# A three-stage fp32 kernel: one pass less when float64 weights are rebuilt, a narrower last product, a new instruction order

## The chip, the cores and the metric

The kernel runs on one core of one Trainium2 chip. Times are device microseconds (us) of one launch. The kernel before takes 1330.62 us, the median of three runs (1329.71 to 1330.99).

## What is computed

Tokens (2 x 4096, 192 channels, float32) pass through three stages:

```
w   = softmax(weight, axis=-1)                # 8 heads, 7 taps
x   = causal_conv(x, w)                       # tap k of head h on its 24 channels
x   = (sigmoid(x @ w_gate) * (x @ w_val)) @ w_out            # 192 -> 1536 -> 192
h   = x @ w_in                                                # 192 -> 2048
P   = a0 + a1*h + a2*h*h + a3*h*h*h
Q   = 1 + |b0|*|h| + |b1|*h*h
out = (P / (Q + 1e-6)) @ w_out2                               # 2048 -> 192
```

The five weight matrices reach the kernel as float64. The result has nearly float32 precision, so each matrix product is made of several TensorE products: both operands are split into a high part (what the fast float32 format fp32r keeps) and a low part (the rest).

## The kernel before, in words

The tokens are cut into 16 tiles of 512. For each tile:

- `conv` makes the seven taps, on POOL for tiles 1 to 15, for tile 0 on TensorE (`conv_first`, 128 channels) and DVE (the other 64), and splits the result into high and low parts (`xha`, `xla`, `xhb`, `xlb`).
- `moe1` makes 12 pairs of 128-row blocks of gate and value. Each block is five TensorE products (`mm192`, L642 to L646: 192 = 128 + 64 channels, high and low parts). ACT applies the sigmoid, DVE multiplies (L688), and for two blocks together (128x1024) `hi1` makes the high part (a copy to fp32r, mostly on ACT) and `lo1` the low part (a subtraction on DVE, L373). Five more products a block, `mm_out` (L649 to L653), add it to `accb`. Of its second accumulator, rows 0 to 63 are the last 64 output channels from the high part of the weight and rows 64 to 127 those from its low part; L653 multiplies that stationary operand with the low part of the data.
- `moe2` makes 16 blocks of `h` with `mm192`; ACT makes `a3*h + a2` (L362, `f<-w,av`) and `|h|`, DVE the polynomial (L753, L755), POOL the denominator's factor (L758), DVE the denominator (L763). The reciprocal is `sigmoid(-log z)`: ACT works on pairs of 128x1024 pieces, first Ln on both, then Sigmoid on both, with a table load on either side. DVE multiplies (L776), `hi2` and `lo2` split, `mm_out` adds to `accd`.

A tile is 340 products of 512 columns (120 + 60 + 80 + 80); 16 tiles make 5440. Ahead of them stand 24 products with zeros (`warm_up`, L599) and the 7 of `conv_first` (L587).

Beside the first tile, 32 pieces of weights are rebuilt. `to_f32` loads pairs of 32-bit words by DMA; ACT rounds the low word's three bits (L444); ACT takes the high word as a float, scales it by 2^-112 and drops its sign (`Abs`); DVE puts the sign bit and the three bits together (L453); DVE shifts the scaled word left by three and puts those bits in (L456). Then a high part (ACT) and a low part (DVE: L373, for the output weights L506 and L508) are made.

The order on every engine is fixed at build time. `Plan` lists the operations with a cost and a priority (`at`: place in time plus an offset by class, `PRM["off"]`), and `Plan.order` goes through model time: the engine that can start soonest takes the operation first in priority. `lock` marks operations of DVE and POOL that the model never lets run at the same time (its shared SBUF port). `alts` lets `hi1`, `hi2` and some copies go to POOL or DVE, with a handicap.

Of the kernel before, what the change touches and what calls it, by code (L numbers as in the profile page):

```python
# [45 lines left out]
class Buf:  # L46
    """A buffer of a kind: the plan gives it a slot, and its first writer its tile."""
# [19 lines left out]
class Plan:  # L67
    """Lists the operations with the buffers that they read and write, then orders them per engine."""
# [6 lines left out]
    def op(self, eng, cost, prio, emit, rd=(), wr=(), table=None, lock=False, alts=()):  # L75
        """alts: other engines that may take the operation, as (eng, cost, emit, lock, handicap)."""
# [32 lines left out]
    def free_slots(self, kind, sort):  # L109
        """Slots of a kind with the time from which each is free, soonest first."""  # L110
# [13 lines left out]
    def fit(self, o):  # L124
        """When the buffers that the operation is first to use can be had, and their slots."""
# [14 lines left out]
    def order(self, look, switch):  # L140
        """In time: the engine that can go on soonest takes, of the operations that it could start
        about then, the one first in priority."""
# [14 lines left out]
        for _ in self.ops:  # L157
            best = None
            for eng in ENGINES:
                found = []  # L160
                for i, o in enumerate(avail[eng]):
                    start = begin(o, eng)
                    if len(o.opts) > 1:
                        ends = {e: begin(o, e) + v[0] + v[3] for e, v in o.opts.items()}
                        if ends[eng] > min(ends.values()):
                            continue
                    found.append((start, o.prio + (switch if o.table and o.table != table else 0.0), i, o))
                found.sort(key=lambda e: e[:3])
                pick, first = None, None
                for start, prio, _, o in found:  # L170
# [14 lines left out]
            o, places, eng = best[1:]  # L185
# [9 lines left out]
            if lock:  # L195
                lock_free = o.end
# [15 lines left out]
        "A": 126, "A.f": -163042, "A.s": 2377, "A.m": 1099, "A.l": 15462, "B": 21954, "B.f": -6649,  # L212
        "B.s": 267339, "B.m": -381, "B.l": 18954, "C": 13792, "C.f": 6615, "C.s": -4092, "C.m": -4326,
        "C.l": -729, "D": 71951, "D.f": 10387, "D.s": -10039, "D.m": 44935, "D.l": 16426, "_": -500387,
        "_.f": -1455, "_.s": -2238, "_.m": -1032, "cb": 85990, "cb.s": 42092, "cb.m": 221, "cb.l": -24842,
        "cv": 108441, "cv.f": 43336, "cv.s": 41633, "cv.l": 5162, "g": -205204, "g.f": -5118, "g.s": 25353,
        "g.m": -7291, "g.l": -9696, "gv": -295099, "gv.f": -7488, "gv.s": 2254, "gv.m": 2921, "ha": 16691,
        "ha.f": -13423, "ha.s": 193315, "ha.m": -32839, "ha.l": 821, "hi1": -34492, "hi1.f": -586,
# [7 lines left out]
        "u.s": 53322, "u.m": -21400, "u.l": 5206, "v": 95617, "v.f": -5614, "v.s": 40813, "v.m": -6140,
        "v.l": 22160, "w": 16438, "w.f": -155676, "w.l": 46096, "wA": -67088, "wA.f": -16171, "wA.s": 4804,
        "wA.m": -6466, "wA.l": -16824, "wB": -72573, "wB.f": 31019, "wB.s": 8326, "wB.m": 53803,
        "wB.l": 1311, "wC": -84679, "wC.s": 22921, "wC.m": 34154, "wC.l": 40145, "wD": 115730,
        "wD.f": 5940, "wD.s": -20677, "wD.m": -48332, "wD.l": 27289, "xs": -442528, "xs.f": -16231,  # L230
# [30 lines left out]
def at(cls, t, x):  # L261
    """Priority of an operation of a class for tile t: its place x in time, moved as the class is."""
# [9 lines left out]
def conv_gated_rational_kernel(  # L272
# [113 lines left out]
    def small():  # L386
# [14 lines left out]
        # exp(z) as sigmoid(z) / sigmoid(-z)  # L401
# [16 lines left out]
        # |b[0]| has a floor far below the rounding of 1, so that the logarithm below stays finite  # L418
# [16 lines left out]
    def to_f32(cls, prio, nbytes, n, load, k=1):  # L435
        """n float64 per partition, as pairs of words, to float32."""
        raw, t = Buf("f", "raw"), Buf("f", "t")

        def words():
# [3 lines left out]
        # the low word's three bits of the float32, rounded  # L443
# [6 lines left out]
        # the high word, its exponent field cut from 11 bits to 8  # L450
        act(at(cls, None, prio + 1), n, lambda: T(t)[:, 0:n], lambda: f(words()[:, :, 1]), [raw], [t],
            func=ACTF.Abs, scale=2.0 ** -112)
        dve(at(cls, None, prio + 2), n, lambda: nc.vector.scalar_tensor_tensor(  # L453
            out=words()[:, :, 0], in0=words()[:, :, 1], scalar=-2 ** 31, in1=words()[:, :, 0],
            op0=ALU.bitwise_and, op1=ALU.bitwise_or), [raw, (raw, 0)], [(raw, 0)])
        dve(at(cls, None, prio + 3), n, lambda: nc.vector.scalar_tensor_tensor(  # L456
            out=T(t)[:, 0:n].bitcast(I32), in0=T(t)[:, 0:n].bitcast(I32), scalar=3, in1=words()[:, :, 0],
            op0=ALU.logical_shift_left, op1=ALU.bitwise_or), [t, (raw, 0)], [t])
        return t

    def split_rows(cls, prio, src, c0, n, hi, lo, key):
        """Columns c0..c0+n of the first 128 rows of a [192, ff] weight."""
# [396 lines left out]
```

## Time and profile before

| what | value |
|---|---|
| median of three runs | 1330.62 us |
| span of the profiled execution, first to last instruction | 1328.7 us |
| PE products, share of the span | 1285.7 us, 97% |
| PE weight loads (overlap the products) | 1032.1 us, 78% |
| DVE | 1238.4 us, 93% |
| ACT | 1162.2 us, 87% |
| POOL | 634.7 us, 48% |
| ACT table loads | 127 of 1.283 us |

The profile gives the span of its execution and no separate time for it. The median of the three runs is 1.9 us above that span; this is what lies around it. A product is pipelined, so the duration of one (about 0.39 us) is longer than the distance from one to the next, and the busy share of PE alone does not say how many products were made. The product count of a stretch, times the distance between two products that do not wait, does.

### The profile page before, as it was taken

What the parts mean: (1) busy time and instruction counts of PE and PEld (TensorE: products, weight loads), DVE (VectorE), ACT (ScalarE), POOL (GpSimd) and SP (SyncE); (2) the same over time, 40 slices, a digit from 0 to 9 for tenths busy, and PEclk for the clock granted to TensorE, in tenths of its full rate; (3) what the DMA queues carried; (4) which work ended last, traced back from release to release, by engine and by line L of the source; (5) the groups of instructions that cost most, each with busy time, mean ns of one, the idle gap of its engine ahead of it and who ended that gap; (6) DMA issues with size and microseconds to landing.
All of it is one profiled execution on the core that took longest, in us unless ns stands there. A gap on an engine that the chain in (4) does not pass through costs nothing.

```text
span 1328.7 us, 15322 instructions
## 1 busy us (share of the span) xinstructions
PE 1285.7 (97%) x5478; PEld 1032.1 (78%) x5478; DVE 1238.4 (93%) x1429; ACT 1162.2 (87%) x1545; POOL 634.7 (48%) x440
## 2 busy tenths in 40 slices
PE   7899799999999999999999999999999999999996
PEld 3767588887888888888888887788888788888874
DVE  8999999999999999999988999999999999999997
ACT  5888889888998889898898889988989888999897
POOL 4035464676355562666517563374644656122222
PEclk8899899999999999999999999999999999999999
DMA  5510100000000000000000000000000000000000
GB/s 166 169 52 25 52 0 21 0 21 9 8 13 1 24 13 1 12 9 21 9 9 5 8 21 9 12 1 17 13 9 13 0 21 1 1 12 1 13 12 12
DMA packets 14316, 27.08 MB, mean 20 GB/s; under 512 B 2080, under 2 KB 5792, under 8 KB 14240
## 3 DMA queue, kind: packets, MB, share of 16 engines
q1 hardware_dynamic: 14240, 26.11, 6.8%
q8 instruction: 43, 0.70, 0.2%
q14 instruction: 33, 0.27, 0.1%
HBM read 19.81 MB, written 6.29 MB: 20 GB/s over the span
## 4 chain that ended last, share of the span: by engine, by line
PE 76%; DVE 14%; ACT 8%; issue 2%; DMA 0%; SPq 0%; DVEq 0%; ACTq 0%
PE w L642 9%; PE w L643 9%; PE w L644 9%; PE w L645 9%; PE w L646 9%; ACT f L362 5%; PE accd L651 4%; PE accd L653 4%; PE accd L652 4%; PE accd L650 4%; PE accd L649 3%; PE accb L651 3%; PE accb L653 3%; PE accb L652 3%; PE accb L649 3%; PE accb L650 3%
## 5 line engine op out<-in xcount | busy, mean ns | idle before, releaser
L758 POOL TENSOR_SCALAR f<-f,bv 128x1024 f32<-128x1024 f32 x128 | 199.0, 1555 | 535.9 <-ACT f L362 479.5
L373 DVE TENSOR_TENSOR r<-f,r 128x1024 fp32r<-128x1024 f32 x224 | 293.2, 1324 | 5.6 <-PE accb L653 1.6
L362 ACT ACTIVATE f<-f 128x1024 f32<-128x1024 f32 (+3 forms) x288 | 285.0, 1004 | 2.8 <-DVE f L763 1.6
L362 ACT ACTIVATE f<-w 128x512 f32<-128x512 f32 x448 | 257.2, 595 | 29.3 <-PE w L646 14.5
L362 ACT ACTIVATE f<-w,av 128x512 f32<-128x512 f32 x256 | 196.7, 774 | 61.5 <-PE w L646 47.6
L362 ACT ACTIVATE r<-f 128x1024 fp32r<-128x1024 f32 x203 | 214.3, 1058 | 26.0 <-DVE f L688 19.8
L755 DVE SCALAR_TENSOR_TENSOR f<-f,av,w 128x512 f32<-128x512 f32 x256 | 187.5, 743 | 8.7 <-ACT f L362 4.4
L753 DVE TENSOR_TENSOR f<-f,w 128x512 f32<-128x512 f32 x256 | 170.7, 680 | 23.0 <-ACT f L362 22.0
L763 DVE SCALAR_TENSOR_TENSOR f<-f,f 128x1024 f32<-128x1024 f32 x128 | 187.9, 1471 | 0.8 <-POOL f L758 0.5
L776 DVE SCALAR_TENSOR_TENSOR f<-f,av,f 128x1024 f32<-128x1024 f32 x128 | 170.4, 1348 | 8.0 <-ACT f L362 7.8
L362 ACT ACT_TABLE_LOAD x126 | 161.7, 1283 | 2.5 <-DVE r L373 0.3
L688 DVE TENSOR_TENSOR f<-f,w 128x512 f32<-128x512 f32 x192 | 130.7, 681 | 23.8 <-PE w L646 13.5
L569 POOL TENSOR_TENSOR ca<-ca,tmp 128x512 f32<-128x512 f32 x90 | 145.5, 1616 | 6.3
L566 POOL TENSOR_SCALAR tmp<-xa,cw 128x512 f32<-128x512 f32 x90 | 124.4, 1382 | 5.5 <-DMA xa<-in_xt 0.5
L651 PE MATMUL accd<-r,wo_s 128*128 128x512 f32 x256 | 102.3, 400 | 5.4 <-DVE r L373 5.3
L650 PE MATMUL accd<-r,wo_s 128*128 128x512 f32 x256 | 101.5, 396 | 4.4 <-DVE wo_s L508 4.4
L649 PE MATMUL accd<-r,wo_s 128*128 128x512 f32 x256 | 101.3, 396 | 3.4 <-ACT r L362 3.3
L642 PE MATMUL w<-yha,w_h 128*128 128x512 f32 x256 | 101.4, 396 | 3.0 <-ACT f L362 2.0
L652 PE MATMUL accd<-r,wo_s 128*128 128x512 f32 x256 | 101.3, 396 | 0.0
L653 PE MATMUL accd<-r,wo_s 128*128 128x512 f32 x256 | 101.3, 396 | 0.0
L644 PE MATMUL w<-yla,w_h 128*128 128x512 f32 x256 | 100.5, 393 | 0.0
L645 PE MATMUL w<-yhb,w_b 128*128 128x512 f32 x256 | 100.4, 392 | 0.0
(104 smaller groups left out, 2861.4 us busy)
## 6 DMA issues: line engine op xcount, KB each, us to landing
f<-in_wo SPq DMA_DIRECT2D x14, 384.0 KB, 3.3
xa<-in_xt SPq DMA_DIRECT2D x16, 259.0 KB, 2.8
out_dram<-f SPq DMA_DIRECT2D x16, 256.0 KB, 2.0
xb<-in_xt SPq DMA_DIRECT2D x16, 129.5 KB, 2.8
f<-in_w SPq DMA_DIRECT2D x4, 512.0 KB, 3.9
out_dram<-f SPq DMA_DIRECT2D x16, 128.0 KB, 2.3
f<-in_wg SPq DMA_DIRECT2D x4, 256.0 KB, 4.2
f<-in_wv SPq DMA_DIRECT2D x4, 256.0 KB, 4.7
```

What stands on the lines that cost most here:

```text
L362: plan.op("ACT", (53 if psum else 95) + n * 0.832 + 93 * ptr, prio, lambda: nc.scalar.activation(out=out(), in_=in_(), func=func, **kw), r ...
L373: dve(prio, n, lambda: nc.vector.tensor_tensor(out=out(), in0=in0(), in1=f(in1()), op=ALU.subtract), rd, wr, lock=lock, alts=alts)
L642: nc.tensor.matmul(o, lhsT=wh.tile[:, c], rhs=ha, start=True, stop=False)
L644: nc.tensor.matmul(o, lhsT=wh.tile[:, c], rhs=la, start=False, stop=False)
L645: nc.tensor.matmul(o, lhsT=wb.tile[:, c], rhs=hb, start=False, stop=False)
L650: nc.tensor.matmul(a1, lhsT=w[:, 2, :], rhs=h, start=False, stop=False)
L651: nc.tensor.matmul(a1, lhsT=w[:, 0, :], rhs=l, start=False, stop=last)
L652: nc.tensor.matmul(a2, lhsT=w[:, 1, :], rhs=h, start=first, stop=False)
L653: nc.tensor.matmul(a2, lhsT=w[:, 1, :], rhs=l, start=False, stop=last)
L755: dve(at("w", t, p), sn, lambda q=q, cut=cut, h=h: nc.vector.scalar_tensor_tensor(out=cut(u[q]), in0=cut(u[q]), scalar=av.tile[:, 1:2], in ...
L758: plan.op("POOL", 328 + 0.832 * gn, at("n", t, p), lambda q=q: nc.gpsimd.tensor_scalar(C(n[q]), C(ha[q]), bv.tile[:, 1:2], bv.tile[:, 0:1] ...
L763: dve(at("y", t, p), gn, lambda q=q: nc.vector.scalar_tensor_tensor(out=C(n[q]), in0=C(ha[q]), scalar=1e-9, in1=C(n[q]), op0=ALU.max, op1= ...
```

## The change

1. `to_f32`: the scaling of the high word is by `Prelu` in place of `Abs`, with alpha = -2^32. A negative word becomes positive and its exponent gets 32 more, a bit that the shift by three moves into the sign's place. DVE's pass L453 falls away, 32 instructions; L456 of before (L461 now) puts in the rounded bits straight from the low word.
2. `mm_out`: the fifth product of a block has 96 stationary columns in place of 128 (416 of the 448; the last block of each accumulation keeps 128). The 32 rows left out would get low part times low part.
3. The order: the model's products take 0.4473 ns a column at full clock in place of 0.422, its shared port is given back 120 ns (DVE) or 140 ns (POOL) before an operation ends and goes to who asked first, and the offsets, handicaps and look-aheads have other values.

The diff, cut (lines taken out of it hold comments and docstrings, and the offsets, whose rows say nothing by themselves):

```diff
+FREES = dict(DVE=120.0, POOL=140.0)
...
-            step = 0.422 if self.cols.get(w - 1, 0.0) >= BUSY else 0.8386
+            step = 0.4473 if self.cols.get(w - 1, 0.0) >= BUSY else 0.8386
...
-                        pick = (key, start, o, places, eng)
-                if pick is not None and (best is None or pick[1] < best[0]):
+                        pick = (key, start, max(asked, t), o, places, eng)
+                if pick is not None and (best is None or pick[1:3] < best[0:2]):
...
             if lock:
-                lock_free = o.end
+                lock_free = max(o.start, o.end - FREES[eng])
...
-    look=dict(PE=0, ACT=0, DVE=19, POOL=31839, SP=0),
-    switch=403355,
+    look=dict(PE=0, ACT=0, DVE=0, POOL=1791, SP=1611),
+    switch=665544,
...
-        hi1=dict(DVE=90316, POOL=72271), hi2=dict(DVE=2766, POOL=113), lo1=dict(POOL=92669),
+        hi1=dict(DVE=380786, POOL=62531),
+        hi2=dict(DVE=73, POOL=0),
+        lo1=dict(POOL=603097),
...
         act(at(cls, None, prio + 1), n, lambda: T(t)[:, 0:n], lambda: f(words()[:, :, 1]), [raw], [t],
-            func=ACTF.Abs, scale=2.0 ** -112)
+            func=ACTF.Prelu, scale=2.0 ** -112, alpha=-2.0 ** 32)
         dve(at(cls, None, prio + 2), n, lambda: nc.vector.scalar_tensor_tensor(
-            out=words()[:, :, 0], in0=words()[:, :, 1], scalar=-2 ** 31, in1=words()[:, :, 0],
-            op0=ALU.bitwise_and, op1=ALU.bitwise_or), [raw, (raw, 0)], [(raw, 0)])
-        dve(at(cls, None, prio + 3), n, lambda: nc.vector.scalar_tensor_tensor(
             out=T(t)[:, 0:n].bitcast(I32), in0=T(t)[:, 0:n].bitcast(I32), scalar=3, in1=words()[:, :, 0],
-            op0=ALU.logical_shift_left, op1=ALU.bitwise_or), [t, (raw, 0)], [t])
+            op0=ALU.logical_shift_left, op1=ALU.bitwise_or), [t, raw], [t])
...
-        nc.tensor.matmul(a2, lhsT=w[:, 1, :], rhs=l, start=False, stop=last)
+
+        m = 128 if last else 96
+        nc.tensor.matmul(a2[0:m], lhsT=w[:, 1, 0:m], rhs=l, start=False, stop=last)
...
-                    plan.op("PE", pe(tn), at("D", t, base + j * Pt / M2), lambda j=j, k=k, c=c: mm_out(
+                    plan.op("PE", pe(tn, 4.943), at("D", t, base + j * Pt / M2), lambda j=j, k=k, c=c: mm_out(
```

How the instructions move is seen in their order on each engine. First DVE at its start, around its first weight passes (`cb` is the convolution of the 64 channels, `wo_s` output weights, `wg_l` the low part of the gate's weights, `f` work buffers). Before:

```order
L453 SCALAR_TENSOR_TENSOR f_129<-f_129 128x256
L561 SCALAR_TENSOR_TENSOR cb_137<-xb_115,cw,cb_137 128x512
L506 TENSOR_TENSOR wo_s<-f_154,wo_s 128x2x64
L508 TENSOR_TENSOR wo_s<-f_154,wo_s 128x2x128
L561 SCALAR_TENSOR_TENSOR cb_137<-xb_115,cw,cb_137 128x512
L456 SCALAR_TENSOR_TENSOR f_158<-f_158,f_129 128x256
L453 SCALAR_TENSOR_TENSOR f_134<-f_134 128x256
L453 SCALAR_TENSOR_TENSOR f_140<-f_140 128x256
L373 TENSOR_TENSOR xlb_187<-cb_137,xhb_179 64x512 x2
L373 TENSOR_TENSOR xla_197<-w_143,xha_191 128x512
L373 TENSOR_TENSOR wg_l<-f_158,wg_h 128x256
```

Now:

```order
L461 SCALAR_TENSOR_TENSOR f_143<-f_143,f_126 128x256
L461 SCALAR_TENSOR_TENSOR f_157<-f_157,f_129 128x256
L566 SCALAR_TENSOR_TENSOR cb_137<-xb_115,cw,cb_137 128x512
L381 TENSOR_TENSOR wg_l<-f_143,wg_h 128x256
L381 TENSOR_TENSOR wg_b<-f_157,wg_b 64x256
L461 SCALAR_TENSOR_TENSOR f_167<-f_167,f_135 128x256
L381 TENSOR_TENSOR wv_b<-f_157,wv_b 64x256
L566 SCALAR_TENSOR_TENSOR cb_137<-xb_115,cw,cb_137 128x512
L381 TENSOR_TENSOR wv_l<-f_167,wv_h 128x256
```

The gate's first low part was the 28th row of DVE's list and is the 17th; the first piece of output weights went ahead of it and now comes behind the first pieces of gate and value. The loads on SP's queue changed places in the same way.

Next PE, at a block of `mm_out` in the first tile (`r` are the high and low parts of the data). Before:

```order
L650 MATMUL accb_354<-r_335,wo_s 128x512
L651 MATMUL accb_354<-r_345,wo_s 128x512
L652 MATMUL accb_355<-r_335,wo_s 128x512
L653 MATMUL accb_355<-r_345,wo_s 128x512
L649 MATMUL accb_354<-r_335,wo_s 128x512
```

Now:

```order
L655 MATMUL accb_340<-r_308,wo_s 128x512
L656 MATMUL accb_340<-r_321,wo_s 128x512
L657 MATMUL accb_341<-r_308,wo_s 128x512
L660 MATMUL accb_341<-r_321,wo_s 96x512
L654 MATMUL accb_340<-r_308,wo_s 128x512
```

The product with 96 columns stands in the place of L653, in front of a product with 128.

Last ACT, at a pair of Ln early in the run (in-place `f` of 128x1024 is Ln behind one table load and Sigmoid behind the next; `f<-w` without `av` is a sigmoid of the gate or an absolute value). Before:

```order
L362 ACT_TABLE_LOAD
L362 ACTIVATE f_1395<-f_1395 128x1024
L362 ACTIVATE f_1468<-w_1513,av 128x512
L362 ACTIVATE f_1491<-f_1491 128x1024
L362 ACTIVATE f_1502<-w_1513 128x512
L362 ACT_TABLE_LOAD
```

Now:

```order
L370 ACT_TABLE_LOAD
L370 ACTIVATE f_1447<-f_1447 128x1024
L370 ACT_TABLE_LOAD
L370 ACTIVATE f_1504<-w_1538 128x512
L370 ACTIVATE f_1567<-w_1528,av 128x512
L370 ACTIVATE f_1572<-w_1528 128x512
L370 ACT_TABLE_LOAD
L370 ACTIVATE f_1477<-f_1477 128x1024
```

A gate's sigmoid now stands between the two Ln of this pair, with a table load on either side; this happens in 14 pairs, so that ACT has 155 table loads in place of 127. Counted over the whole order, ACT makes 170 high parts of 128x1024 in place of 203, POOL 40 in place of 21, and DVE 14 in place of none.

## Rows read from the trace of the kernel before

**Rows 1.** Page, part 1: busy us, share of the span, instructions of each engine.

```profile
PE 1285.7 (97%) x5478; PEld 1032.1 (78%) x5478; DVE 1238.4 (93%) x1429; ACT 1162.2 (87%) x1545; POOL 634.7 (48%) x440
```

**Rows 2.** Windows: length, busy us (instructions) of each engine, granted clock, DMA.

```profile
17.00:180.00 163.00, 140.93 (x547) 108.70 (x547) 154.81 (x212) 131.69 (x212) 70.96 (x51) 0.92 0.27 79
...
22.00:24.00 2.00, 2.00 (x6) 1.52 (x6) 2.00 (x4) 1.77 (x5) 1.86 (x2) 0.50 1.05 365
...
180.00:1270.00 1090.00, 1086.30 (x4721) 884.19 (x4721) 1022.87 (x1137) 973.88 (x1257) 549.68 (x375) 1.00 0.04 10
1270.00:1328.70 58.70, 45.05 (x175) 33.66 (x173) 49.01 (x56) 47.99 (x59) 13.34 (x9) 0.94 0.05 14
```

**Rows 3.** Timeline of PE from 600 us: start us, us, engine, line, instruction.

```profile
600.21 0.39 PE L652 MATMUL accb<-r,wo_s 128*128 128x512 f32 x1
...
611.65 0.39 PE L652 MATMUL accd<-r,wo_s 128*128 128x512 f32 x1
```

**Rows 4.** Waits of PE, 17 to 180 us: us in total, times, longest.

```profile
PE accd L650 <- DVE wo_s L508: 4.4, 1, 4.4
...
PE accb L651 <- DVE r L373: 2.7, 2, 1.4
```

**Rows 5.** Groups by line and form, DVE, 0 to 200 us: busy, mean ns | idle before.

```profile
L453 DVE SCALAR_TENSOR_TENSOR f<-f 128x384 int32<-128x384 int32 x14 | 11.1, 817 | 0.0
L453 DVE SCALAR_TENSOR_TENSOR f<-f 128x512 int32<-128x512 int32 x12 | 9.5, 811 | 0.0
...
L453 DVE SCALAR_TENSOR_TENSOR f<-f 128x256 int32<-128x256 int32 x6 | 3.2, 562 | 0.0
```

**Rows 6.** Line L453: ns min/median/max, first and last start.

```profile
L453 DVE SCALAR_TENSOR_TENSOR f<-f x32: 423/680/1786, 9.8 to 175.8; 128x384 int32<-128x384 int32 x14, 128x512 int32<-128x512 int32 x12, 128x256 int32<-128x256 int32 x6
```

**Rows 7.** Timeline of DVE, from 9.8 us.

```profile
9.77 0.56 DVE L453 SCALAR_TENSOR_TENSOR f<-f 128x384 int32<-128x384 int32 x1
10.23 0.75 DVE L561 SCALAR_TENSOR_TENSOR cb<-xb,cw,cb 128x512 f32<-128x512 f32 x1
```

**Rows 8.** Timeline of PE's weight loads: products with bf16 zeros, at full clock.

```profile
4.94 0.31 PEld L599 LDWEIGHTS <-zeros 128*128 128x128 bf16 x2
...
7.31 0.31 PEld L599 LDWEIGHTS <-zeros 128*128 128x128 bf16 x2
```

**Rows 9.** The same, fp32r products at half clock.

```profile
22.16 0.33 PEld L645 LDWEIGHTS w<-xhb,wv_b 128*128 128x128 f32 x1
...
23.87 0.33 PEld L644 LDWEIGHTS w<-xla,wg_h 128*128 128x128 f32 x1
```

**Rows 10.** Lines L653 and L599: ns min/median/max of the weight loads.

```profile
L653 PEld LDWEIGHTS accd<-r,wo_s x256: 187/188/330, 119.6 to 1323.2; 128*128 128x128 f32 x128
...
L599 PEld LDWEIGHTS <-zeros x24: 98/98/151, 1.3 to 7.7; 128*128 128x128 bf16 x24
```

**Rows 11.** Line L362 on ACT, 180 to 1270 us: ns min/median/max.

```profile
L362 ACT ACTIVATE f<-w x389: 575/596/645, 185.5 to 1269.4; 128x512 f32<-128x512 f32 x195
...
L362 ACT ACTIVATE f<-w,av x226: 752/777/814, 183.9 to 1269.9; 128x512 f32<-128x512 f32 x113
```

**Rows 12.** Timeline of ACT in the tail.

```profile
1304.58 1.04 ACT L362 ACTIVATE f<-f 128x1024 f32<-128x1024 f32 x1
1305.64 1.28 ACT L362 ACT_TABLE_LOAD   x1
1306.93 2.01 ACT L362 ACTIVATE f<-f 128x1024 f32<-128x1024 f32 x2
```

**Rows 13.** Line L358 on POOL, and two groups by line of DVE.

```profile
L358 POOL TENSOR_SCALAR r<-f x21: 1044/1053/1914, 162.5 to 1311.4; 128x1024 fp32r<-128x1024 f32 x21
...
L373 DVE TENSOR_TENSOR r<-f,r 128x1024 fp32r<-128x1024 f32 x224 | 293.2, 1324 | 5.6 <-PE accb L653 1.6 <-PE accb L652 1.1 <-ACT f L362 0.8
...
L558 DVE TENSOR_SCALAR cb<-xb,cw 128x512 f32<-128x512 f32 x1 | 0.5, 488 | 2.3 <-DMA xb<-in_xt 2.3
```

**Rows 14.** Waits of ACT, 180 to 1270 us.

```profile
ACT f L362 <- PE w L646: 52.9, 66, 2.6
```

More of the change, by code (lines that the diff above doesn't have):

```diff
@@ L166, in order @@
                             continue
-                    found.append((start, o.prio + (switch if o.table and o.table != table else 0.0), i, o))
+                    found.append((start, o.prio + (switch if o.table and o.table != table else 0.0), i, o,
+                                  max(free[eng], o.ready)))
                 found.sort(key=lambda e: e[:3])
                 pick, first = None, None
-                for start, prio, _, o in found:
+                for start, prio, _, o, asked in found:
                     if first is not None and start > first + look[eng]:
@@ L211 @@
     off={
[L212 to L216, printed above, removed]
@@ L226 @@
[L226 to L230, printed above, removed]
@@ L231 @@
-        "xs.s": 13914, "xs.m": -15171, "xs.l": -39981, "y": -355208, "y.f": -7695, "y.s": 1663,
-        "y.m": 24499, "ye": -431004, "ye.f": -15550, "ye.s": 821, "ye.m": 9621, "ye.l": 20452,
-        "late": -1636,
-    },
-    look=dict(PE=0, ACT=0, DVE=19, POOL=31839, SP=0),
-    switch=403355,
+        "A": -639, "A.f": -1063628, "A.s": 3849, "A.m": -5402, "A.l": 20648, "B": 24359, "B.f": 101,
+        "B.s": 722765, "B.m": -6951, "B.l": 152716, "C": 10166, "C.f": 10448, "C.s": 11168, "C.m": -1283,
@@ new lines @@
+        "C.l": -258574, "D": 70387, "D.f": -2028, "D.s": -614, "D.m": 1145112, "D.l": -70882, "_": -500387,
+        "_.f": -1455, "_.s": -2238, "_.m": -1032, "cb": 77111, "cb.s": 42092, "cb.m": 106261, "cb.l": -24842,
+        "cv": 141808, "cv.f": 43336, "cv.l": 41643, "g": 930, "g.f": 58060, "g.s": -73181, "g.m": -13081,
+        "g.l": -42561, "gv": -280594, "gv.f": -114326, "gv.s": 107189, "gv.m": -100720, "ha": 62917,
+        "ha.f": 87796, "ha.s": 256, "ha.m": -14101, "ha.l": 381418, "hi1": -87178, "hi1.f": -6018,
[4 rows of a table added]
@@ new lines @@
+        "n.l": 199703, "oe": 102172, "oe.f": -59209, "oe.s": -590, "oe.m": 47437, "oe.l": 152139, "r": 171267,
+        "r.f": -146955, "r.s": 18933, "r.l": 76895, "sig": -27281, "sig.f": -741190, "sig.s": -143913,
+        "sig.m": -3296, "sig.l": 100824, "u": 731, "u.f": 2963, "u.s": 20903, "u.m": 589, "v": 266828,
+        "v.f": -61171, "v.s": 29097, "v.m": 35890, "v.l": -18955, "w": -98481, "w.f": 16961, "w.l": 47711,
+        "wA": -104549, "wA.f": -16171, "wA.s": 4804, "wA.m": -6466, "wA.l": -16824, "wB": -95021,
@@ new lines @@
+        "wB.f": 31019, "wB.s": 8326, "wB.m": 53803, "wB.l": 1311, "wC": -86460, "wC.s": 22921, "wC.m": 34154,
+        "wC.l": 40145, "wD": 515662, "wD.f": 5940, "wD.s": -20677, "wD.m": -48332, "wD.l": 27289,
+        "xs": -656637, "xs.f": 544, "xs.s": 4476, "xs.m": 7392, "xs.l": 440853, "y": -620020, "y.f": 9273,
+        "y.s": 1832, "y.m": -58874, "ye": -212572, "ye.s": 103292, "ye.m": 164438, "ye.l": -156589,
+        "late": 9141, "ld.f": -2869, "lo2.s": -448302, "gv.l": -86635, "w.s": -107106, "cb.f": 23472,
@@ L237 @@
+        "cv.m": -98167, "y.l": -369111, "w.m": 30924, "hi2.f": -154, "ln.l": -3795, "ld.l": 342338,
+        "r.m": -95445,
+    },
+    look=dict(PE=0, ACT=0, DVE=0, POOL=1791, SP=1611),
+    switch=665544,
     slots=dict(f=12, r=7, y=1),
@@ L239 @@
     alt=dict(
-        hi1=dict(DVE=90316, POOL=72271), hi2=dict(DVE=2766, POOL=113), lo1=dict(POOL=92669),
-        lo2=dict(POOL=17018), n=dict(DVE=86223), round=dict(DVE=34164),
-        xy=dict(DVE=67223, POOL=15669),
+        hi1=dict(DVE=380786, POOL=62531),
+        hi2=dict(DVE=73, POOL=0),
+        lo1=dict(POOL=603097),
+        lo2=dict(POOL=222218),
+        n=dict(DVE=1362960),
+        round=dict(DVE=1027190),
+        xy=dict(DVE=562408, POOL=308632),
     ),
@@ L695, in moe1 @@
                 c = slice(i % g * n, (i % g + 1) * n)
-                plan.op("PE", pe(n), at("B", t, base + i * Pt / M1), lambda i=i, h=h, l=l, c=c: mm_out(
+                plan.op("PE", pe(n, 4.943), at("B", t, base + i * Pt / M1), lambda i=i, h=h, l=l, c=c: mm_out(
                     T(a1)[:, 0:n], T(a2)[:, 0:n], wo_s.tile[:, i], T(h)[:, c], T(l)[:, c], i == 0, i == M1 - 1),
```

7 lines of the change are left out of this document (1 added, 6 removed), and 8 rows, old and new, of the table off.

## The prediction

> **What bounds the kernel now.** The page's first part [rows 1] says PE 97%, DVE 93%, ACT 87%: three engines near full, so the share does not decide, and a busy PE may be waiting inside a product. The timeline of PE in an undisturbed stretch [rows 3] gives the distance between products: 50 products from 600.21 to 611.65 us, 0.229 us each. With it the windows [rows 2] tell the time lost in a stretch, its length less products times 0.229. From 17 to 180 us 547 products need 125.3 of 163 us: 37.7 us lost. From 180 to 1270 us 4721 products need 1081 of 1090: 9 lost. From 1270 us to the end 175 need 40.1 of 58.7: 18.6 lost. So the middle is bound by PE, and the losses lie in the head, where the weights are rebuilt, and in the tail, where the last tile's chain runs out.
>
> In the head DVE is busy 154.8 of 163 us [rows 2] and the longest waits of PE there end with it: a low part of the output weights, a low part of the data [rows 4]. Each loss also pulls the clock down (mean granted share 0.92 there against 1.00 in the middle [rows 2]). What DVE need not do before a product, PE gets back; and as the middle is PE's, what is gained in the head stays gained to the tail.
>
> **One pass less.** L453 runs 32 times, 14, 12 and 6 by size, for 11.1 + 9.5 + 3.2 = 23.8 us [rows 5], all between 9.8 and 176 us [rows 6]: the whole pass lies in the head, on the engine that bounds it. Not all of it need come back. The mean of 0.81 us for 512 elements holds waiting in front of POOL's work; the median of all is 0.68, the least 0.42 [rows 6], and the next instruction starts 0.10 before one ends (0.56 us long, next start after 0.46 [rows 7]). Undisturbed, the passes cost 14 x 0.46 + 12 x 0.58 + 6 x 0.32 = 15.3 us. ACT's pass stays one pass: Sigmoid and Abs share the group `f<-w` and all of it lies between 575 and 645 ns [rows 11], so I cost Prelu in Abs's place at nothing. If its alpha were fetched as the two per-partition operands of `f<-w,av` are, it would cost as much as 777 - 596 = 181 ns a pass, 32 x 0.18 = 6 us, on an ACT that is idle 31 of 163 us there [rows 2]. The low word now waits for two ACT passes of its own piece only, and nothing stands between.
>
> **The order in the head.** Counted in the two orders, the rows that DVE must issue for a low part in front of a given product fall from 182 to 159 (about 445 products in), from 201 to 172 (about 510), from 266 to 236 (about 700), from 278 to 254 (about 770) and from 338 to 304 (about 970). These 23 to 34 rows hold the passes removed and some work put off (output weights of the second layer). At 154.8 / 212 = 0.73 us a row they are 17 to 25 us. The first weights also come earlier: the gate's low part is DVE's 17th row, was the 28th; on SP's queue its load is ahead of the output weights' first. I take 22 us. The lower end is 12: the 15.3 us less some 3 that DVE will now idle, as ACT and the loads are nearer behind it. The upper end is 28: the 25 us with some of the time that the half clock cost; PE can't get back more than 37.7.
>
> **The 96 columns.** An fp32r weight load takes 188 ns at full clock, a bf16 one 98 [rows 10]. The bf16 products follow each other after (7.31 - 4.94) / 11 = 0.2155 us [rows 8], the fp32r ones after 0.229 [rows 3]. At half clock (1.2 GHz; granted share 0.50 from 22 to 24 us [rows 2]) the fp32r load takes 0.33 and its products come after (23.87 - 22.16) / 4 = 0.43 us [rows 9], which is 512 columns at 1.2 GHz. So the extra 13.5 ns show only where load plus some 40 ns is longer than the stream of columns: the load sets the distance. From half to full clock it falls by 330 - 188 = 142 ns, the part that goes with the clock; a quarter fewer columns take 36 ns off, 188 + 41 - 36 = 193 ns, below 215.5. So the distance in front of each of 416 products becomes 0.2155: 416 x 0.0135 = 5.6 us. Ends: 0, if the 13.5 ns belong to fp32r streams and not to loads, and 5.6. No row shows a product of fewer columns; that it could cost more than one of 128 has nothing for it in the trace. [...]
>
> **The middle.** ACT gets 28 more table loads. A load takes 1.28 us, starts 0.02 us after the instruction before it ends and the next starts 0.01 after it [rows 12]: 1.29 us, 28 x 1.29 = 36 us. 33 high parts of some 0.95 us leave ACT, 31 us. Net 5 us of the 116 in which ACT is idle between 180 and 1270 us [rows 2]; it waits there for PE for 52.9 us [rows 14], so it has time. The Trainium skill, "ScalarE: Activation LUTs", section "What ACT_TABLE_LOAD costs", counts 1.38 us of draining on top of 1.28 for each switch; by it 28 switches would be 39 us more of ACT, and the rival of the split pairs below would cost up to 75 us, not 36. The trace shows no such gap. DVE gets 14 copies of 1024 elements, of between 0.49 us (512 elements, L558) and 1.32 (L373 at 1024) [rows 13], 7 to 18 us, I take 9, and the 17 to 25 us put off or brought nearer by the head: some 31 of its 67 idle us [rows 2]. POOL gets 19 copies of 1.05 us [rows 13], 20 us, in 540 idle ones. All three still fit, but with less play; I take 3 us more lost, between 0 and 12.
>
> **The tail.** ACT is busy 48.0 and DVE 49.0 of 58.7 us [rows 2]. Both orders reach the last tile's fifth block after the same 5275 products; from there ACT has 64 rows where it had 66, DVE the same kinds. Behind the last block's products PE has 60 `mm_out` products left, had 70. I take 1 us less, between 5 less and 4 more.
>
> **Sum.** -22 - 5.6 + 3 - 1 = -25.6. The profiled span of 1328.7 becomes 1303.1, and with the 1.9 us that the median lies above it, 1305.0 us.
>
> **Rivals.**
> *The head stays bound* (12 us gained, not 22): ACT and the loads take DVE's place. Against it: ACT is busy 131.7 of 163 us there [rows 2], 81%. For it: each weight piece is a chain of load, two ACT passes, DVE, ACT, DVE, and a shorter DVE shows the rest. 1305 + 10 = 1315 us.
> *The narrow product gives nothing*: 1305 + 5.6 = 1310.6 us. For it only that no row shows fewer columns.
> *The split pairs of Ln reach PE*: in 14 pairs the second Ln comes behind a gate's sigmoid and two loads, so two reciprocals, their high and low parts and 20 `mm_out` products come 2.6 us later or more. If PE paid the 28 loads in full, 36 us: 1341 us, slower than before. It decides when PE pays over 25.6 of the 36, about 0.9 us a load. Against it: between 180 and 1270 us PE has other blocks to go on with, it lost 9 us in all there with 114 loads.
> *The rest*: an order whose model fits better also loses less in the middle and the tail, 1290 us or below; or DVE's put-off work comes up short in the middle, 1320 us and more.
>
> **How the numbers follow.** Forecast, 0.58, its own range 1295 to 1313. Head still bound 0.16. Nothing from the 96 columns 0.10. Split pairs reach PE 0.06 (of it 0.04 slower than before). The rest 0.10, 0.05 on either side. The range of eight in ten takes the forecast with its ends, the narrow product's rival and most of the first: 1291 to 1320. A measurement of this kernel tells some 0.2%, 2.7 us, from no change. Faster by more: all but what lies above 1328, 0.92. Within: 0.03. Slower: 0.05.
>
> **What would show it.** Right: between 17 and 180 us over 620 products in place of 547; no L453; the distance in front of the 96-column product 0.215 to 0.217 us and a load of some 0.15 us; 155 table loads with waits of PE between 180 us and the tail of under 12 us; a tail as long as before. Wrong in the head: fewer than 600 products there, with DVE no longer at 95% and waits of PE that end with ACT or a DMA. Wrong on the columns: 0.229 in front of L660. Wrong altogether: waits of PE behind ACT in the middle that sum to more than 25 us.

## The result, and the profile after

The changed kernel takes 1338.95 us, median of four runs (1337.27 to 1340.15); the kernel before, beside it, 1330.16. The ratio is 1.0065, 95% interval 1.0051 to 1.0079: slower by 0.65%, where 1305 us was forecast. The profiled execution's span is 1336.5 us.

The page's first part, answering to [rows 1]:

```profile
PE 1299.0 (97%) x5478; PEld 1017.2 (76%) x5478; DVE 1220.8 (91%) x1411; ACT 1166.3 (87%) x1540; POOL 661.1 (49%) x459
```

The windows, answering to [rows 2] (length, busy us and instructions of PE, PEld, DVE, ACT, POOL, granted clock, DMA):

```profile
17.00:180.00 163.00, 153.41 (x640) 119.04 (x641) 154.96 (x203) 141.57 (x224) 91.75 (x66) 0.99 0.26 76
180.00:1270.00 1090.00, 1078.70 (x4596) 852.96 (x4596) 999.54 (x1124) 964.07 (x1232) 546.70 (x374) 1.00 0.03 10
1270.00:1336.50 66.50, 53.18 (x206) 39.73 (x204) 55.99 (x62) 51.74 (x64) 21.88 (x14) 0.90 0.04 12
```

The head did what was forecast: 640 products in place of 547, 93 x 0.229 = 21.3 us, with DVE as busy as before. The loss is in the middle: 4596 products in place of 4721, at the full clock. With the prediction's measure, length less products times 0.229, the middle now loses 1090 - 1052.5 = 37.5 us, where it lost 9.

Two things fill these 37.5 us. PE's timeline shows the first (start us, us, engine, line, instruction):

```profile
399.89 0.40 PE L657 MATMUL accb<-r,wo_s 128*128 128x512 f32 x1
400.13 0.40 PE L660 MATMUL accb<-r,wo_s 128*96 128x512 f32 x1
400.36 0.40 PE L647 MATMUL w<-yha,w_h 128*128 128x512 f32 x1
...
402.46 0.40 PE L660 MATMUL accd<-r,wo_s 128*96 128x512 f32 x1
```

and the timeline of its weight loads:

```profile
399.89 0.16 PEld L660 LDWEIGHTS accb<-r,wo_s 128*96 128x96 f32 x1
400.13 0.19 PEld L647 LDWEIGHTS w<-yha,w_h 128*128 128x128 f32 x1
```

From 399.89 to 402.46 us are 11 distances, 0.2336 each, in place of 0.229 [rows 3]. The narrow load is shorter as forecast (0.16 us against 0.19), but its product starts no earlier: 0.24 us behind the one before. And every other product, all of 128 columns, is later too.

The second is waits. In the waits of DVE between 180 and 1270 us (us in total, times, longest) stands after the change

```profile
DVE f L760 <- ACT f L370: 37.4, 47, 3.5
DVE f L695 <- ACT f L370: 13.1, 17, 2.4
```

and before it

```profile
DVE f L753 <- ACT f L362: 22.0, 42, 1.3
...
DVE f L688 <- ACT f L362: 6.4, 11, 1.4
```

L760 is L753 of before, the polynomial's first multiplication, and L695 is L688, the gate's. To set the two apart, all starts of products were counted in PE's order: distances under 0.25 us are running (their excess over 0.229 is "distance"), those of 0.40 to 0.432 are half clock, and the excess of the rest is "waits". Each of these columns has the value before and after.

| products | before | after | distance | half clock | waits |
|---|---|---|---|---|---|
| 0 to 38 (start) | 15.3 | 17.6 | -0.2, -0.2 | 4.0, 4.5 | 2.8, 4.5 |
| 38 to 700 (head) | 189.8 | 166.3 | 0.1, 1.5 | 8.7, 1.4 | 29.4, 11.8 |
| 700 to 5282 (middle) | 1058.5 | 1086.9 | -0.2, 15.9 | 0.0, 0.0 | 9.4, 21.7 |
| 5282 to 5477 (tail) | 58.5 | 59.0 | 0.1, 0.4 | 1.8, 3.0 | 12.0, 11.0 |

The sum is +2.3 - 23.5 + 28.4 + 0.5 = +7.7 us; the spans differ by 1336.5 - 1328.7 = 7.8.

### The profile page after: what moved, and what is told of

Read it like the earlier page. It is cut to its first block, busy times and chain, and to the rows that moved or that the text cites. A ratio compares the mean times of both kernels' runs of the same rounds, so it can differ in the third digit from the quotient of the medians.

```text
span 1336.5 us, 15377 instructions
## 1 busy us (share of the span) xinstructions
PE 1299.0 (97%) x5478; PEld 1017.2 (76%) x5478; DVE 1220.8 (91%) x1411; ACT 1166.3 (87%) x1540; POOL 661.1 (49%) x459
## 4 chain that ended last, share of the span: by engine, by line
PE 44%; DVE 23%; ACT 22%; issue 6%; POOL 3%; DMA 0%; SPq 0%; ACTq 0%; DVEq 0%; POOLq 0%
ACT f L370 13%; PE w L647 5%; PE w L651 5%; PE w L649 5%; PE w L648 5%; PE w L650 5%; DVE r L381 4%; ACT L370 4%; DVE f L760 4%; DVE f L762 4%; DVE f L783 3%; DVE f L770 3%; ACT r L370 3%; PE accd L656 2%; DVE f L695 2%
## 5 line engine op out<-in xcount | busy, mean ns | idle before, releaser
L765 POOL TENSOR_SCALAR f<-f,bv 128x1024 f32<-128x1024 f32 x128 | 185.1, 1446 | 482.0 <-ACT f L370 375.8
L381 DVE TENSOR_TENSOR r<-f,r 128x1024 fp32r<-128x1024 f32 x224 | 299.0, 1345 | 7.9 <-PE accd L660 2.4
L760 DVE TENSOR_TENSOR f<-f,w 128x512 f32<-128x512 f32 x256 | 172.0, 681 | 42.7 <-ACT f L370 42.1
L370 ACT ACTIVATE r<-f 128x1024 fp32r<-128x1024 f32 x170 | 179.0, 1058 | 35.9 <-DVE f L695 22.7
L762 DVE SCALAR_TENSOR_TENSOR f<-f,av,w 128x512 f32<-128x512 f32 x256 | 188.8, 744 | 13.3 <-ACT f L370 9.0
L770 DVE SCALAR_TENSOR_TENSOR f<-f,f 128x1024 f32<-128x1024 f32 x128 | 178.2, 1393 | 7.3 <-POOL f L765 7.3
L783 DVE SCALAR_TENSOR_TENSOR f<-f,av,f 128x1024 f32<-128x1024 f32 x128 | 176.6, 1392 | 8.2 <-ACT f L370 7.9
L695 DVE TENSOR_TENSOR f<-f,w 128x512 f32<-128x512 f32 x192 | 130.5, 680 | 16.2 <-ACT f L370 14.4
L656 PE MATMUL accd<-r,wo_s 128*128 128x512 f32 x256 | 103.6, 405 | 6.4 <-DVE r L381 6.4
L654 PE MATMUL accd<-r,wo_s 128*128 128x512 f32 x256 | 102.3, 400 | 0.6 <-ACT f L370 0.6
L651 PE MATMUL w<-ylb,w_b 128*128 128x512 f32 x256 | 101.7, 397 | 0.6 <-DVE ylb L381 0.6
L655 PE MATMUL accd<-r,wo_s 128*128 128x512 f32 x256 | 102.0, 398 | 0.0
L660 PE MATMUL accd<-r,wo_s 128*96 128x512 f32 (+1 forms) x256 | 101.7, 397 | 0.0
L657 PE MATMUL accd<-r,wo_s 128*128 128x512 f32 x256 | 101.6, 397 | 0.0
```

Source lines behind the costliest of these rows:

```text
L370: plan.op("ACT", (53 if psum else 95) + n * 0.832 + 93 * ptr, prio, lambda: nc.scalar.activation(out=out(), in_=in_(), func=func, **kw), r ...
L381: dve(prio, n, lambda: nc.vector.tensor_tensor(out=out(), in0=in0(), in1=f(in1()), op=ALU.subtract), rd, wr, lock=lock, alts=alts)
L651: nc.tensor.matmul(o, lhsT=wb.tile[:, c], rhs=lb, start=False, stop=True)
L695: dve(at("gv", t, p), n, lambda sc=sc, val=val: nc.vector.tensor_tensor(out=sc(), in0=sc(), in1=val(), op=ALU.mult), [(pv, "v"), (s, i)], ...
L760: dve(at("v", t, p), sn, lambda q=q, cut=cut, h=h: nc.vector.tensor_tensor(out=cut(u[q]), in0=cut(u[q]), in1=h(), op=ALU.mult), [ps_, (u[q ...
L762: dve(at("w", t, p), sn, lambda q=q, cut=cut, h=h: nc.vector.scalar_tensor_tensor(out=cut(u[q]), in0=cut(u[q]), scalar=av.tile[:, 1:2], in ...
```

## The experiments

Theory N: the narrow product slows PE. Theory S: the split pairs of Ln with their loads make PE wait. All runs in one table (e11 is one run alone), each ratio against the kernel before on the same chip; "lost" is 1090 us less products times 0.229, between 180 and 1270 us.

| run | us | ratio to before, interval | products 17 to 180 us | 180 to 1270 us | lost |
|---|---|---|---|---|---|
| before | 1330.16 | | 547 | 4721 | 8.9 |
| the change | 1338.95 | 1.0065, 1.0051 to 1.0079 | 640 | 4596 | 37.5 |
| e1 | 1334.1 | 1.0037, 1.0024 to 1.005 | 642 | 4615 | 33.2 |
| e2 | 1346.13 | 1.0117, 1.01 to 1.0134 | 544 | 4658 | 23.3 |
| e3 | 1319.88 | 0.9931, 0.9914 to 0.9948 | 597 | 4721 | 8.9 |
| e4 | 1384.43 | 1.0414, 1.0398 to 1.0429 | 636 | 4429 | 75.8 |
| e5 | 1312.24 | 0.9867, 0.9852 to 0.9882 | 636 | 4713 | 10.7 |
| e6 | 1346.67 | 1.0126, 1.0106 to 1.0145 | 577 | 4614 | 33.4 |
| e7 | 1336.96 | 1.0057, 1.0039 to 1.0076 | 641 | 4601 | 36.4 |
| e8 | 1317.71 | 0.9909, 0.9894 to 0.9924 | 647 | 4669 | 20.8 |
| e9 | 1364.94 | 1.0256, 1.0239 to 1.0274 | 639 | 4488 | 62.2 |
| e10 | 1333.73 | 1.0031, 1.0018 to 1.0044 | 637 | 4614 | 33.4 |
| e11 | 1330.23 | | 554 | 4718 | 9.6 |
| e12 | 1328.73 | 0.9993, 0.9983 to 1.0003 | 593 | 4698 | 14.2 |

**e1: the change with 128 columns; e2: the kernel before with 96.** Orders as in the change and as before; e2 leaves out the same low times low sums as the change.

```diff
-        m = 128 if last else 96
+        m = 128
```

> The changed kernel with 128 columns in every fifth product, all else and the order of every engine the same. Theory N (the narrow product switches PE from 229 to 233 ns between products, and it stays there until PE waits): mean distance of running products back to 229 ns, 17 to 18 us less, 1321 us. Rival O (the order, or what the other engines do beside PE, sets the distance): distance stays at 232 ns, time within 3 us of 1339 us.

> The kernel before with 96 columns in the fifth product, order of every engine unchanged. Theory N: distance rises from 229 to 232 ns or more over 5440 products, 1330 + 15 to 20 = 1345 to 1350 us. Rival O: distance unchanged at 229 ns, or 0.2155 us in front of the 416, 1325 to 1331 us.

The windows of e1, then of e2:

```profile
180.00:1270.00 1090.00, 1072.02 (x4615) 860.56 (x4614) 999.90 (x1126) 964.76 (x1235) 549.81 (x374) 1.00 0.03 10
```

```profile
180.00:1270.00 1090.00, 1088.31 (x4658) 867.69 (x4657) 1013.28 (x1123) 963.07 (x1238) 537.09 (x373) 1.00 0.04 10
```

In the order before, 96 columns alone cost 16.1 us, as N has it: the middle's distance grows by 18.0 us (mean 232.9 ns in place of 229.0), its waits fall from 9.4 to 5.6. In e1 the distance is back at 229.1, but the waits of the middle rise from 21.7 to 32.3 us, so only 4.9 us come back, where N had 17 to 18. With PE at its old pace the new order is not bound by PE in the middle. The waits of PE in e1, 180 to 1270 us:

```profile
PE w L647 <- DVE f L762: 5.0, 9, 1.6
PE accb L654 <- DVE yla L381: 4.5, 5, 1.6
PE accd L656 <- DVE r L381: 2.8, 4, 1.2
PE w L647 <- ACT f L370: 2.6, 6, 0.6
```

Many small ones behind DVE: L762, whose end frees a buffer of `w`, and low parts (L381). This view counts idle time alone, 18.0 us in all (1090 - 1072.02); the 32.3 us hold more, as a product can start late while the one before it, 0.39 us long, has not ended. Nor is DVE fuller: per product of PE it is busy 0.2167 us there in both orders (999.90 / 4615, and 1022.87 / 4721 before). What it does more of is wait for ACT:

```profile
DVE f L760 <- ACT f L370: 38.5, 47, 3.6
```

**e3: the kernel before without the sign pass, its order kept.**

```diff
-            func=ACTF.Abs, scale=2.0 ** -112)
-        dve(at(cls, None, prio + 2), n, lambda: nc.vector.scalar_tensor_tensor(
-            out=words()[:, :, 0], in0=words()[:, :, 1], scalar=-2 ** 31, in1=words()[:, :, 0],
-            op0=ALU.bitwise_and, op1=ALU.bitwise_or), [raw, (raw, 0)], [(raw, 0)])
+            func=ACTF.Prelu, scale=2.0 ** -112, alpha=-2.0 ** 32)
+        dve(at(cls, None, prio + 2), n, lambda: None, [raw, (raw, 0)], [(raw, 0)])
```

> The kernel before without the DVE pass that puts the sign in (Prelu makes it), order of every engine otherwise unchanged. If DVE bounds the head and the middle is PE's: 15 to 24 us of DVE removed come back, less what ACT and the loads hold up, 1307 to 1318 us, with the waits and half-clock products of the head falling from 38 us to some 20. Rival (the order made the head faster, not the pass): under 6 us gained, 1325 us or more.

The windows of e3:

```profile
17.00:180.00 163.00, 147.35 (x597) 114.86 (x597) 147.33 (x198) 140.97 (x224) 79.36 (x57) 0.96 0.27 80
180.00:1270.00 1090.00, 1086.26 (x4721) 884.09 (x4720) 1023.91 (x1135) 973.75 (x1259) 545.35 (x373) 1.00 0.04 10
```

The pass alone gives 50 products, 11.5 us, and the middle is untouched. (The time is 2 us above its expectation: the head's waits and half-clock products fall to 26.8 us, not 20.) The rest of the head's gain (640 products against 597, 9.8 us) is the new order's. This kernel beats both.

**e4: e1 with the first Ln of every pair moved down to the second.** 128 table loads in place of 155.

```diff
+    for o in order:
+        if o.table == "ln" and held is None:
+            held = o
+            continue
+        joined += [held, o] if o.table == "ln" else [o]
...
```

> The changed kernel with 128 columns, and in every pair the first Ln moved down to stand directly in front of the second, so that no table load falls between them; all other instructions in the same order. Theory S (the split pairs, 26 table loads more on ACT, make PE wait in the middle): waits of PE in the middle fall from some 22 to some 10 us, 8 to 14 us less than the kernel with 128 columns alone. Rival P (the put-off DVE work and the copies moved to DVE and POOL make PE wait): within 3 us of the kernel with 128 columns alone.

Fewer loads, and 50 us more: S fell as it was put, and P's 3 us did not hold either. But this moved the first Ln of whole pairs too, behind work that stood between; e7 is the cleaner cut.

**e5 and e6: the two orders spliced.** What one plan starts ahead of a point goes in that plan's order, all the rest in the other's (`SEQ` holds the two lists; the kernel follows them engine by engine).

```diff
-    order = plan.order(K["look"], K["switch"])
+    order = follow(plan)
...
```

> Products of 128 columns, no sign pass. Every operation that the changed kernel's plan starts in its first 250 us stands in that plan's order and on its engine; all others stand in the order and on the engines of the kernel before. Theory O (the order of the middle is at fault, and the gain of the head is the head's own): head as in the changed kernel, 166 us for products 38 to 700 (before 190), middle as before with about 9 us of waits, so 1330 - 23.5 + 1 or 2 = 1306 to 1310 us. Rival D (the head's gain is a debt: work is put off that the middle has to pay): the middle's waits are 20 us or more again, and the time is 1320 us or more.

> The other way round: products of 128 columns, no sign pass; what the plan of the kernel before starts in its first 160 us stands in that order, all others in the order of the changed kernel. Theory O: the middle's waits of PE are 25 to 35 us though the head puts nothing off, the head takes about 178 us as in the kernel before without the sign pass, so 1320 + 22 = about 1342 us. Rival D: the middle's waits are 9 to 12 us, and the time is 1320 to 1324 us.

The windows of e5:

```profile
17.00:180.00 163.00, 153.21 (x636) 120.08 (x637) 154.76 (x203) 141.67 (x223) 92.42 (x66) 0.98 0.26 74
180.00:1270.00 1090.00, 1085.07 (x4713) 882.39 (x4712) 1024.34 (x1144) 975.57 (x1262) 540.84 (x366) 1.00 0.03 10
```

and of e6:

```profile
180.00:1270.00 1090.00, 1071.22 (x4614) 860.34 (x4613) 996.67 (x1127) 959.69 (x1228) 561.96 (x383) 1.00 0.04 10
```

Head and middle come apart: with the new head and the old middle the loss in the middle is 10.7 us, with the old head and the new middle 33.4, as in e1. So the waits go with the middle's own order; they are no debt of the head. (e6 ends 5 us above its expectation because its head takes 183.3 us, not 178.) In e5 DVE waits at L760 for ACT as little as before:

```profile
DVE f L760 <- ACT f L370: 20.9, 38, 1.5
```

e5 is the fastest kernel of all, 1.3% under the kernel before. It ends 2 us above its expectation: the head takes 167.2 us, the middle 1060.3 (+1.8), and its start 17.7 (+2.4), which the expectation had left out.

**e7: e1 with only the split pairs joined.** A first Ln moves down only where another table's operation stands between; 129 loads.

```diff
+        if o.table == "ln" and held is None:
+            nxt = next(p for p in order[i + 1:] if p.eng == "ACT" and p.table)
+            held = o
+            if nxt.table == "ln":
+                joined.append(o)
...
+        if o.table == "ln":
+            joined += [held, o] if moved else [o]
...
```

> The changed kernel with 128 columns (1334.1 us, waits of PE in the middle 32 us), and of a pair of Ln between which another table's operation stands on ACT the first is moved down to the second; the whole pairs stay: 129 table loads in place of 155. Theory S (the split pairs and their loads cause the waits): the waits of the middle fall to 15 us or less, about 1316 us. Rival T (the place of the pairs counts, not their loads): within 5 us of 1334 us, or longer, as the first Ln now comes onto the way of the second.

The windows of e7:

```profile
180.00:1270.00 1090.00, 1070.54 (x4601) 860.00 (x4600) 999.14 (x1127) 933.36 (x1209) 545.04 (x374) 1.00 0.03 10
```

ACT has 31 us less to do there than in e1 (964.76), and PE gains nothing: 36.4 us lost against 33.2. S's number falls, and T's holds (2.9 us from 1334). What ACT saves it spends waiting, 20 us of it for PE. ACT's largest sum of waits in the middle, in e1 and then in e7:

```profile
ACT f L370 <- PE w L651: 46.2, 37, 3.0
```

```profile
ACT f L370 <- PE w L651: 66.5, 53, 3.0
```

Whether the later place of the first Ln takes back what the loads give is not told apart here; e8 takes the loads out without moving anything.

**e8: e1 with Abs in place of Ln,** which leaves out the logarithm and needs no table of its own.

```diff
-                    func=ACTF.Ln, table="ln", scale=1.0 / ONE)
+                    func=ACTF.Abs, table="ln", scale=1.0 / ONE)
```

> The changed kernel with 128 columns and Abs in place of Ln, which needs no table of its own: 1 load in place of 155, orders the same. The second layer's gate is left without its logarithm. ACT has 154 x 1.28 = 197 us less to do. Theory A (PE's waits in the middle go back to ACT: DVE is late because ACT is late): waits fall below 10 us, so about 1334 - 22 = 1312 us or less. Rival V (DVE itself is too full or its order serves the wrong operation first): waits stay at 20 us or more, time over 1322 us.

The windows of e8:

```profile
180.00:1270.00 1090.00, 1081.40 (x4669) 873.69 (x4668) 1016.72 (x1143) 803.40 (x1115) 563.43 (x379) 1.00 0.03 10
```

Without any load in the middle and with ACT 161 us lighter, 12 of the 33 us come back and 20.8 stay lost; of these 3.8 are a longer distance between products, the counted waits are 15.6. The number lies between the two theories: ACT's time has a share in the waits, but even an ACT with 287 idle us does not cure this order. DVE waits at L760 nearly as long as in e1 (38.5), and ACT itself now waits for PE's products:

```profile
DVE f L760 <- ACT f L370: 34.5, 42, 2.3
```

```profile
ACT f L370 <- PE w L651: 125.9, 114, 3.1
```

So DVE's wait for ACT is a link in a ring (PE waits for DVE, DVE for ACT, ACT for PE), and not only a sign that ACT has too much to do.

**e9: e1 with the second layer's high parts on the engines of before,** 33 more on ACT, places in the queues kept.

```diff
...
+        for i in those.split():
+            o = plan.ops[int(i)]
+            o.eng, o.emit = eng, o.opts[eng][1]
```

> The changed kernel with 128 columns, its queues in their order, but each of the 52 high parts of the second layer that the two plans give to different engines stands on the engine of the kernel before: 29 go from POOL and 13 from DVE to ACT, 10 to POOL (9 of them from ACT). Theory E (the high parts on POOL and DVE make the middle wait: they take 1.3 and 0.74 us against 1.06 on ACT, and DVE's copies lie on a full engine): the middle's waits fall from 32 to 20 us or less, about 1320 us. Rival Q (it is the place in the queues, whatever engine copies): the waits stay within 8 us of 32 or grow, as ACT, on which DVE waits, gets some 33 more passes: 1330 us or more.

In the windows of e9

```profile
180.00:1270.00 1090.00, 1050.57 (x4488) 837.83 (x4487) 974.68 (x1090) 966.23 (x1233) 524.04 (x357) 1.00 0.03 10
```

the loss nearly doubles, 62.2 us. Theory E falls: the copies on POOL and DVE were no burden but a relief. DVE's wait at L760 grows with it:

```profile
DVE f L760 <- ACT f L370: 52.5, 58, 3.8
```

**e12: the same kind of load on the old order.** e3 with its 21 high parts of POOL moved to ACT.

```diff
+        if o.eng == "POOL" and getattr(o.prio, "cls", "") == "hi2":
+            o.eng, o.emit = "ACT", o.opts["ACT"][1]
```

> The kernel before without the sign pass (1319.88 us, waits of PE in the middle 9.4 us), and the 21 high parts of the second layer that stand on POOL there moved to ACT, in their places: about 21 us more of work for ACT. In the order of the changed kernel 33 more passes on ACT cost PE 27.5 us of waits, 0.83 us each. Theory M (the order before has play between ACT, DVE and PE that the new one has used up): at most 0.4 us each, waits under 18 us, 1328 us or less. Rival K (ACT is as tight in both orders, and the new one loses by something else): 0.8 us each, waits of 26 us or more, 1336 us or more.

The windows of e12:

```profile
180.00:1270.00 1090.00, 1082.78 (x4698) 879.14 (x4697) 1016.74 (x1128) 984.30 (x1271) 517.39 (x355) 1.00 0.04 10
```

The middle loses 14.2 us in place of 8.9. Of the 21 passes 18 lie in it: 0.29 us each. In e9 25 of the 33 lie in the middle (its ACT made 169 such parts beside 4488 products, e1's 148 beside 4615): (62.2 - 33.2) / 25 = 1.16 us each, more than a pass takes. So in the middle a pass put on ACT costs the old order a quarter of what it costs the new one, as M has it: the old order has play there that the new one lacks. The whole time, 1328.73, is 0.7 above M's bound, as the tail pays 2.8 us too (61.7 against 58.9 for its products). The two runs are not quite alike: e9 moves other passes and also takes 13 copies from DVE, so the size of the difference is not settled by them.

**e10: 64 columns in place of 96** (32 more rows of sums left out); **e11: the kernel before with six single products of 96 columns.**

```diff
-        m = 128 if last else 96
+        m = 128 if last else 64
```

```diff
+        done[0] += 1
+        m = 96 if done[0] % 60 == 30 and not last else 128
```

> The changed kernel with 64 columns in place of 96 in the last product of a block (32 of the low rows' sums are left out). Theory N (any product that does not fill the columns upsets the rhythm of loads and products, and it stays upset until PE next waits): again about 232.5 ns from product to product in the middle, 1339 us within 5. Rival W (what counts is how much the load is shortened, and 96 was not short enough): the distance in front of the narrow product falls to about 216 ns or the 229 ns come back around it, and the time is 1334 us or less.

> The kernel before with six single products of 96 columns, some 200 us apart, all others of 128. Theory N: from each of the six the distance is 233 ns in place of 229 and stays so until PE next waits, some 50 to 100 products and 0.2 to 0.4 us each; six such stretches, time as before within 3 us. Rival L (only the products beside the narrow one are longer, by its own load): 229 again from the second product behind it.

With 64 columns the 229 ns are back (mean 229.1 in the middle), 33.4 us lost as in e1, and the time is e1's within 0.4 us. Line L660's weight loads in e10 (ns min/median/max, then first and last start), and its timeline of PE:

```profile
L660 PEld LDWEIGHTS accd<-r,wo_s x221: 133/134/188, 183.8 to 1267.7; 128*64 128x64 f32 x97, 128*128 128x128 f32 x14
```

```profile
599.66 0.39 PE L647 MATMUL w<-yha,w_h 128*128 128x512 f32 x1
...
604.00 0.39 PE L660 MATMUL accb<-r,wo_s 128*64 128x512 f32 x1
...
611.10 0.39 PE L647 MATMUL w<-xha,wv_h 128*128 128x512 f32 x1
```

A load of 134 ns, and still no shorter distance: 50 products from 599.66 to 611.10 us, three of them narrow, 0.2288 each. So of these two widths N holds for 96 alone, and W's mechanism fell too: the distance is back at 229, no product came sooner, and nothing is gained. In e11 (1330.23 us) five of the six single products left no lasting trace, and one did. The one at 509 us, and the one at 1177:

```profile
509.13 0.39 PE L654 MATMUL accb<-r,wo_s 128*128 128x512 f32 x1
509.36 0.39 PE L657 MATMUL accb<-r,wo_s 128*96 128x512 f32 x1
509.59 0.39 PE L642 MATMUL w<-xha,wg_h 128*128 128x512 f32 x1
```

```profile
1176.81 0.39 PE L654 MATMUL accb<-r,wo_s 128*128 128x512 f32 x1
1177.05 0.40 PE L657 MATMUL accb<-r,wo_s 128*96 128x512 f32 x1
1177.28 0.40 PE L651 MATMUL accd<-r,wo_s 128*128 128x512 f32 x1
...
1206.21 0.40 PE L657 MATMUL accb<-r,wo_s 128*128 128x512 f32 x1
```

From 1177.05 to 1206.21 us are 125 distances of 0.2333 us with no other narrow product among them, and it goes on so to about 1242 us. So one product can set the slower pace for 65 us, and another of the same form does nothing (N forecast six such stretches and one came, L none). What decides is told below.

## Why the prediction was wrong

Its own steps, one by one:

- **One pass less, and the order in the head: right.** -22 us forecast; -23.5 in products 38 to 700. e3 puts 11.3 us of it on the pass (189.8 to 178.5; the step's undisturbed 15.3 less some 3 was 12), the rest on the order. `Prelu` at nothing was right: the passes take 554 and 669 ns for 384 and 512 elements, Abs took 554 and 662. What it left out is the start, 2.3 us: PE's first real product now waits 3.8 us for ACT's `xha`.
- **The 96 columns: wrong, in sign.** The step said that the load sets the distance and "that it could cost more than one of 128 has nothing for it in the trace": -5.6 us, between 0 and -5.6. Measured, in the order before: +16.1 (e2); in the new order 4.9 (e1). Loads of 163 and 134 ns in place of 188 bring no product forward. The inference from half clock was the fault: load and distance both changed there with the clock, so no row told them apart. The rival "gives nothing" was nearer, and what a 64-column product does (e10). The Trainium skill, "TensorE: Matmul & The Clock Gate", section "Back-to-back issue gap", gives N / 2.4 + 2.5 ns for an isolated product, an estimate of 215.8 ns for 512 columns, and says that in a stream of loads and products both set the spacing, some 131 ns for 512 columns. Here the bf16 products with zeros come at 215.5 ns beside their loads [rows 8]; no fp32r row shows either figure (229 and 233 ns), and with a load cut to 134 ns the spacing stayed at 229 (e10).
- **The middle: mis-sized, and the largest miss.** +3 forecast, 12 at most; the new order makes 22.9 us more waits at the old pace (e1, 32.3 against 9.4), 12.3 beside the slower products. The step added up busy time and found that "all three still fit, but with less play". Busy time did fit: DVE is idle 90 us and ACT 126 there, more than before. But each engine takes its queue in order, and DVE stands at L760 for ACT more often and longer (37.4 us against 22.0), then PE behind DVE. The step priced work and left out these waits. That they come with the order of the middle is shown by e5 and e6; that they are the way in which it costs PE time is read from the waits, and no run removed them alone.
- **The rival of the split pairs: right place, but not by the cause that it named.** Its sign, "slower than before", came true, and waits in the middle were its sign; but joined pairs (e7) cure nothing, and with no load at all in the middle (e8) the new order still waits 15.6 us, where the order before waits 9.4 with all of its loads. So the 28 loads can't be the whole of what PE pays for; their own share was not measured apart (e8 gave back 12 us for all the loads together). That the loss lies in the middle's order is shown by e5 and e6; that this order has less play is what e9 and e12 point to.
- **The tail: right**, +0.5 for -1.

In sum, by the counted products: without the narrow product the change is worth +1.8 (start) - 23.5 (head) + 24.4 (middle, 1082.9 against 1058.5; 22.9 of it waits) + 0.7 (tail) = +3.4 us, the +3.5 of e1's span. The narrow product adds 4 in the middle: 15.3 of distance, less 10.6 of waits, as a slower PE seems to wait less (in e2 too, 5.6 against 9.4), and 0.7 of half clock. Against the forecast of -25.6 the middle's order is 21 us too long, the narrow product about 10 and the start 2.

Still open: which of the scheduler's new numbers (the pace of 0.4473 ns a column, the port given back early, the offsets) took the play out of the middle was not tried apart; any of them gives another order everywhere.

## What to carry to other kernels

An order can be good in one stage and bad in the next: count the products of each stage, then splice the orders; here that gave 1312 us with 128 columns (e5), better than either kernel. Where engines run above 85% and wait for each other in order, ask what a late result costs in the queue behind it, not whether the busy times still fit. And a smaller operation is not a cheaper one until a trace shows it: try it alone in the old order first.

## What the hardware showed that was not expected

fp32r products of 512 columns run at full clock in one of two rhythms: a beat of three distances, 226, 229 and 232 ns (mean 229.0), or an even 233.3 ns. Either holds for hundreds of products. What a product of 96 columns does goes by its place in the beat. In e2's middle, 38 of them met the beat with no wait near:

- Eight came where the beat has 226 as the distance to the narrow product itself; they left the beat as it was.
- Thirteen came where the beat has 229. The distance to them was 235 or 236, and five products further on the beat was back.
- Seventeen came where the beat has 232. The distance to them was 233 or 234, and from there on it was 233, mostly until PE next waited.

The six of e11 do the same: four stood in the first place, one (1015.87 us) in the second, and the one at 1177.05 us in the third. Of some 300 in e2 that met the 233, all but four left it as it was. In e10 nearly all of some 290 products of 64 columns that met the beat left it alone, in whatever place.

The slower pace is not the narrow product's alone. Kernels with 128 columns in every product fall into it too, though seldom: e7 for some 500 products in four stretches, and e8 twice, once for over 700 products with no wait among them. PE in e8:

```profile
553.89 0.40 PE L651 MATMUL w<-xlb,wg_b 128*128 128x512 f32 x1
...
725.62 0.40 PE L654 MATMUL accd<-r,wo_s 128*128 128x512 f32 x1
```

These are 736 distances of 0.2333 us; they are most of e8's 3.8 us of distance. The kernel before and e1 show no such stretch. The pattern is counted in the traces; what in PE makes it, and what else than a narrow product sets the slower pace, is not settled.
